# A decode block with cached attention and a gated MLP: x in eight loads, W_o in three, and the gate products on h itself

## The chip, the cores and the metric

The kernel runs on one core of one Trainium2 chip. The core has a matrix engine (PE), three engines for elementwise work (DVE, ACT and POOL), a queue engine (SP) that issues most of the loads, and 16 DMA engines that carry them out. The metric is the device time of one execution in microseconds.

## The reference

Two tokens (B = 2, one position each) of width 512 go through one block. The attention has 32 heads of width 128, each with its own cached keys and values of 8192 positions:

```python
h = x + attention(layernorm(x)) @ wo
#   q = layernorm(x) @ wq;  p = softmax(q k / sqrt(128));  attention = p v
n = layernorm(h)
gate = n @ W_gate;  up = n @ W_up          # 512 -> 1376
out = h + (gate * (gate > 0) * up) @ W_down
```

Everything comes in as bfloat16. Keys and values are 268 MB of the 281 MB that the kernel reads; W_q and W_o are 4.2 MB each, and the three MLP weights 1.4 MB each.

## The kernel before, in words

The order of all instructions on every engine is the order of the program text (a manual schedule). The framework adds the waits. It gives each DMA one of eight completion semaphores, named DMAHW0 to DMAHW7, in turn; a DMA that takes a semaphore again is preceded by a wait for the DMA that had it before.

*Front.* x comes in as five small loads issued by ACT (L190), each a piece of one token's row in one partition. SP issues W_q, the first K tile and the first V tile right behind each other (L193, L165). x is transposed on PE, `ln_cols` (L169) makes its layernorm, and 32 products (L252) make q, which is spread over the partitions as `qrep`. DVE meanwhile reduces the identity matrix into small selection matrices `quot` and `rest` (L243, L244).

*Caches.* Four heads of one token are a step: a K tile and a V tile of 8 MB each, in three rotating buffers of 8 MB. In each step DVE multiplies most of K by q (`products`, L375) and adds up by halves (`scores`, L393 and L395), while PE and ACT do the rest of the rows (`scores_pe`); the exponentials follow, and PE multiplies them by V (`values`, L446). SP issues the next V when the scores have freed K's buffer and the next K but one when `values` has freed V's buffer. The last four heads of the second token are two half steps, p0 and p1, of 4 MB tiles; p1's values are taken with V as the weights (`values_cols`, L469), in two halves.

*W_o.* The attention result of a head is a column `ocol` of 128 values. For a set of n heads, `spread` and `lay_rows` (L492, L496) lay these columns out in `orow` so that W_o can be read with n * 512 values of consecutive rows in each partition, and `attend_set` (L502) multiplies them. Before, the sets are 16, 8, 4 and 2 heads (`SETS`), and the last two heads (HM = 30 and 31), which come last from p1, are loaded one by one and multiplied without the layout, by `attend` (L509). That makes six loads of W_o (L567, L589, L590). The first is issued ahead of p1's V, the others right behind it.

*MLP.* W_gate, W_up and W_down follow in SP's queue (L612, L616, L621), W_down in seven pieces. `hc` (L659) is h in columns, in float32. Its mean is a product with a constant matrix (L661), `hn` is h minus its mean in bfloat16 (L666), and `through` (L686) multiplies 11 chunks of 128 rows of W_gate by `hn`. The variance is applied behind the products. Meanwhile h is split into three bfloat16 parts `hb` (L674 to L677), which PE transposes into `hrow` (L695) for adding h back. Then come W_up's products, `hm` (L727), the products with W_down (`down`, L719), two copies and the store (L736).

Of the kernel before, what the change touches and what calls it, by code (L numbers as in the profile page):

```python
# [8 lines left out]
ALU = mybir.AluOpType  # L9
AXIS = mybir.AxisListType  # L10
# [3 lines left out]
def _free(t, offset, dims):  # L14

    return bass.AP(tensor=t.tensor, offset=t.offset + offset, ap=[t.ap[0]] + [list(d) for d in dims])


def _dram(t, offset, dims):
    return bass.AP(tensor=t.tensor, offset=t.offset + offset, ap=[list(d) for d in dims])  # L20
# [3 lines left out]
def kernel(  # L24
# [13 lines left out]
    nc = tc.nc  # L38
    P = nc.NUM_PARTITIONS
    B, Sq, D = A_x.shape  # L40
    _, Hkv, Sk, Dh = A_k_cache.shape
    Hq = A_wq.shape[1] // Dh
    F = B_W_gate.shape[1]
    KC = D // P
    EPS = 1e-5
    SCALE = float(Dh) ** -0.5
    bf16 = mybir.dt.bfloat16
    f32 = mybir.dt.float32
# [16 lines left out]
    QZ = 32  # L65


    SETS = [(0, 16, 0), (16, 8, 16), (24, 4, 24), (28, 2, 28)]
    HM = 30
    SROWS = [n for _, n, _ in SETS]  # L70


    FSETS = [(0, 5), (5 * P, 3), (8 * P, 1), (9 * P, 1), (F - P, 1)]
    FC = 11
# [7 lines left out]
    consts = ctx.enter_context(tc.tile_pool(name="consts", bufs=1))  # L82
    small = ctx.enter_context(tc.tile_pool(name="small", bufs=1))
    ps = ctx.enter_context(tc.tile_pool(name="ps", bufs=1, space=PSUM))
    ps2 = ctx.enter_context(tc.tile_pool(name="ps2", bufs=2, space=PSUM))

    qTs = front.tile([P, B, Hq], bf16)
    ocol = front.tile([P, Hq, B], bf16)
# [16 lines left out]
    ident = consts.tile([P, P], bf16)  # L105
# [3 lines left out]
    mean_w = consts.tile([P, P], f32)  # L109
    eps_col = consts.tile([P, 1], f32)  # L110
    warm = consts.tile([P, 1], f32)
    hm = consts.tile([P, FC, B], bf16)
    quot = {r: consts.tile([P, Dh // r], bf16, name=f"quot{r}") for r in SROWS}
    rest = {r: consts.tile([P, r], bf16, name=f"rest{r}") for r in SROWS}
    orow = [consts.tile([P, r, B], bf16, name=f"orow{k}") for k, r in enumerate(SROWS)]
    sel = consts.tile([B, B, P // 2], bf16)
    xc = consts.tile([P, B, KC], f32)
# [7 lines left out]
    wo = bufs[0][:, HALF:TILE]  # L125
# [60 lines left out]

    with tc.manual_schedule():

        for b, k, n in ((0, 0, 2), (0, 2, 2), (1, 0, 2), (1, 2, 1), (1, 3, 1)):
            nc.scalar.dma_start(  # L190
                out=xr[b:b + 1, k * P:(k + n) * P], in_=_dram(A_x, b * D + k * P, [[D, 1], [1, n * P]]),
            )
# [46 lines left out]
        nc.vector.tensor_copy(xc, x_ps.rearrange("p c b -> p b c"))  # L239
        xn = small.tile([P, KC, B], bf16, tag="xn")  # L240
        ln_cols(xc, xn.rearrange("p c b -> p b c"), "l1")
        for r in SROWS:
            nc.vector.tensor_reduce(out=rest[r], in_=_free(ident, 0, [[1, r], [r, P // r]]), axis=AXIS.X, op=ALU.max)  # L243
            nc.vector.tensor_reduce(out=quot[r], in_=_free(ident, 0, [[r, P // r], [1, r]]), axis=AXIS.X, op=ALU.max)  # L244
        nc.scalar.activation(out=warm, in_=eps_col, func=ACT.Exp)
# [230 lines left out]
        def spread(k, b):  # L476

            h0, n, _ = SETS[k]
            nq = Dh // n
            sp = qrep[:, B * k + b, :]  # L480
            nc.vector.tensor_tensor(
                out=_free(sp, 0, [[nq, n], [1, nq]]), in0=_free(ocol, h0 * B + b, [[B, n], [0, nq]]),
                in1=_free(quot[n], 0, [[0, n], [1, nq]]), op=ALU.mult,
            )
            return sp

        def lay_rows(k, sps, scalar=False):

            r = SROWS[k]
            or_ps = ps.tile([P, B, r], f32, tag="mx")  # L490
            for b in range(B):
                nc.tensor.matmul(out=or_ps[:, b, :], lhsT=sps[b], rhs=rest[r], start=True, stop=True)  # L492
            if scalar:
                nc.scalar.activation(out=orow[k], in_=or_ps.rearrange("p b c -> p c b"), func=ACT.Copy)
            else:
                nc.vector.tensor_copy(orow[k], or_ps.rearrange("p b c -> p c b"))  # L496

        def attend_set(k, r0=0, r1=None):
            for c0 in range(r0, SROWS[k] if r1 is None else r1):
                for c in range(KC):  # L500
                    at = (SETS[k][2] + c0) * D + c
                    nc.tensor.matmul(  # L502
                        out=att_ps[:, c, :], lhsT=_free(wo, at, [[KC, P]]), rhs=orow[k][:, c0, :],
                        start=(k == 0 and c0 == 0 and c == 0), stop=False, skip_group_check=True,
                    )

        def attend(h):
            for c in range(KC):
                nc.tensor.matmul(  # L509
                    out=att_ps[:, c, :], lhsT=_free(wo, h * D + c, [[KC, P]]), rhs=ocol[:, h, :],  # L510
                    start=False, stop=(h == Hq - 1), skip_group_check=True,
                )

        place_q(steps[0])
        for i in range(Q):
# [70 lines left out]
        load_tile(A_v_cache, p1, p1.vt)  # L586
        for k in range(1, len(SETS)):
            load_set(k)
        nc.sync.dma_start(out=wo[:, HM * D:(HM + 1) * D], in_=_dram(A_wo, HM * Dh * D, [[D, P], [1, D]]))  # L589
        nc.sync.dma_start(  # L590
            out=wo[:, (HM + 1) * D:Hq * D], in_=_dram(A_wo, (HM + 1) * Dh * D, [[P // 4 * D, 4], [D, P // 4], [1, D]]),
        )
        scores(p0)

        def first():
# [24 lines left out]
            fc = f0 // P  # L620
            nc.sync.dma_start(out=wd_sb[:, fc:fc + n, :], in_=_dram(B_W_down, f0 * D, [[n * D, P], [1, n * D]]))  # L621
        late = bufs[1][:, HALF + D:HALF + D + P + D]
        hrow, parts3 = late[0:3 * B, 0:D], late[0:3 * B, D:D + B]
        hb = late[:, D + 32:D + 32 + 3 * B * KC].rearrange("p (c k b) -> p c k b", c=KC, k=3)
        hlow = late[:, D + 64:D + 64 + 2 * B * KC].bitcast(f32).rearrange("p (c b) -> p c b", c=KC)
        nb = heads(Q)[2]
        rzs[Q] = small.tile([P, nb], f32, tag="both", name="both")
# [9 lines left out]
        diagonals(Q)  # L637
        exponentials(p1)
        normalise(Q)
        sps = [[spread(k, b) for b in range(B)] for k in range(1, len(SETS))]  # L640
        nc.gpsimd.tensor_tensor(out=parts3, in0=ident[0:3 * B, 0:B], in1=ident[0:3 * B, B:2 * B], op=ALU.add)  # L641
        nc.gpsimd.tensor_tensor(out=parts3, in0=parts3, in1=ident[0:3 * B, 2 * B:3 * B], op=ALU.add)
        half = p1.nt // 2
        values_cols(p1, 0, half)
        for k in range(1, len(SETS)):
            lay_rows(k, sps[k - 1])
        nc.vector.memset(wd_sb[0:AGAIN, FC - 1, :], 0.0)
        sums(Q + 2)
        shares(Q + 2)
        values_cols(p1, half, p1.nt)  # L650
        normalise(Q + 2)
        for k in range(1, len(SETS)):
            attend_set(k)
        for h in range(HM, Hq):
            attend(h)

        nc.vector.tensor_tensor(out=hc, in0=att_ps.rearrange("p c b -> p b c"), in1=xc, op=ALU.add)  # L659
        m_ps = ps.tile([P, B, KC], f32, tag="mx")  # L660
        nc.tensor.matmul(out=m_ps, lhsT=mean_w, rhs=hc, start=True, stop=True)  # L661
        mean = small.tile([P, B], f32, tag="l1mean")
        nc.vector.tensor_reduce(out=mean, in_=m_ps, axis=AXIS.X, op=ALU.add)
        hn = small.tile([P, KC, B], bf16, tag="hn")
        mean_b = _free(mean, 0, [[1, B], [0, KC]])
        nc.vector.tensor_tensor(out=hn.rearrange("p c b -> p b c"), in0=hc, in1=mean_b, op=ALU.subtract)  # L666
        dev = small.tile([P, B, KC], f32, tag="l1dev")
        nc.vector.tensor_tensor(out=dev, in0=hc, in1=mean_b, op=ALU.subtract)
        sq = small.tile([P, B, KC], f32, tag="l1sq")
        nc.vector.tensor_tensor(out=sq, in0=dev, in1=dev, op=ALU.mult)  # L670


        hcc = hc.rearrange("p b c -> p c b")
        nc.vector.tensor_copy(hb[:, :, 0, :], hcc)  # L674
        nc.vector.tensor_tensor(out=hlow, in0=hcc, in1=hb[:, :, 0, :], op=ALU.subtract)
        nc.vector.tensor_copy(hb[:, :, 1, :], hlow)
        nc.vector.tensor_tensor(out=hb[:, :, 2, :], in0=hlow, in1=hb[:, :, 1, :], op=ALU.subtract)  # L677

        chunks = [(f0 + c, n) for f0, n in FSETS for c in range(n)]
        UP = 5  # L680

        def through(w_ps, k, part, cs=range(KC)):
            for fc in part:
                f0, n = chunks[fc]
                for c in cs:
                    nc.tensor.matmul(  # L686
                        out=w_ps[:, fc - part[0], :], lhsT=_free(wgu[:, k, c, :], f0, [[n, P]]), rhs=hn[:, c, :],
                        start=(fc == part[0] and c == 0), stop=(c == KC - 1), skip_group_check=True,
                    )

        g_ps = ps.tile([P, FC, B], f32, tag="row")
        through(g_ps, 0, range(FC))
        hT_ps = ps2.tile([3 * B, KC, P], bf16, tag="o")
        for c in range(KC):
            nc.tensor.transpose(hT_ps[:, c, :], hb[:, c].rearrange("p k b -> p (k b)"), ident)  # L695
        nc.scalar.activation(
            out=hrow.rearrange("q (p c) -> q p c", c=KC), in_=hT_ps.rearrange("q c p -> q p c"), func=ACT.Copy,
        )
        v_ps = ps.tile([P, B, KC], f32, tag="mx")
        nc.tensor.matmul(out=v_ps, lhsT=mean_w, rhs=sq, start=True, stop=True)  # L700
        rvar = small.tile([P, B], f32, tag="l2rvar")
        nc.vector.tensor_reduce(out=rvar, in_=v_ps, axis=AXIS.X, op=ALU.add)
        nc.vector.tensor_scalar_add(rvar, rvar, EPS)
        nc.vector.reciprocal(out=rvar, in_=rvar)
        gate = small.tile([P, FC, B], f32, tag="gate")
        nc.vector.scalar_tensor_tensor(
            out=gate, in0=g_ps, scalar=0.0, in1=_free(rvar, 0, [[0, FC], [1, B]]), op0=ALU.max, op1=ALU.mult,
        )
        parts = [(range(0, UP), "of", ps), (range(UP, FC), "tp", ps2)]
        u_ps = [pool.tile([P, len(part), B], f32, tag=tag, name="u_ps") for part, tag, pool in parts]  # L710
# [11 lines left out]
                )  # L722

        for t, (part, _, _) in zip(u_ps, parts):
            through(t, 1, part)
            f = slice(part[0], part[-1] + 1)
            nc.vector.tensor_tensor(out=hm[:, f, :], in0=gate[:, f, :], in1=t, op=ALU.mult)  # L727
        down(parts3, hrow, start=True)
# [38 lines left out]
```

## Time and profile before

| | |
|---|---|
| runs | 659.56, 658.91, 659.28 us; median 659.28 |
| span of the profiled execution | 657.5 us, 1.8 us less than the median of the runs |
| busy: DVE, PE, PE weight loads, ACT, POOL | 558.1, 352.1, 158.9, 123.6, 24.1 us |
| read from HBM | 281.05 MB, 427 GB/s over the span |
| share of the loads' queue in the time of 16 DMA engines | 99.1% |

The span begins with the first recorded instruction and ends with the last. "SPq" and "ACTq" are DMA issues by SP and ACT. A line `start length engine line op out<-in xcount [idle before <-releaser]` is one group of instructions in order of time. The chain that ended last is followed back from the end, from each step to what released it; a piece `DMA tile<-in_...` in it lasts from the load's issue to its landing, including the time in which it stood behind other loads.

### The profile page before, as it was taken

To read this page: it belongs to the slowest core of one execution; us is meant where nothing else is said; L and a number is where in the kernel's file an instruction comes from. 1 tells how busy PE (TensorE), PEld (TensorE's weight loads), DVE (VectorE), ACT (ScalarE), POOL (GpSimd) and SP (SyncE) were. 2 spreads that over 40 slices of the span, in tenths; PEclk is the share of its full clock that TensorE was granted. 3 is DMA by queue.
4 is the path that set the end of the run, shared out by engine and by line. 5 is a ranking of instruction groups with operands and counts; after the bars stand their busy time and mean duration, and the time that the engine had idled before them with its cause. 6 is when DMAs were issued, how large, how long until landed. Compare 5 with 4: busy or idle time off the path is not lost.

```text
span 657.5 us, 5117 instructions
## 1 busy us (share of the span) xinstructions
PE 352.1 (54%) x2118; PEld 158.9 (24%) x2118; DVE 558.1 (85%) x252; ACT 123.6 (19%) x337; POOL 24.1 (4%) x36
## 2 busy tenths in 40 slices
PE   0730934809175380926539092552918458291997
PEld 0310311304022130312204031220403224030456
DVE  0599697988979799897979989796997969999982
ACT  0230030200203020030301103030210304201870
POOL 3080000000000000000000000000000000000020
PEclk9975775958778596877959687695968869686895
DMA  9999999999999999999999999999999999999997
GB/s 383 447 444 447 387 440 443 447 399 444 439 443 436 419 436 435 439 439 436 423 443 424 439 440 427 447 416 443 439 423 440 423 443 436 423 444 413 425 425 291
DMA packets 6948, 281.37 MB, mean 428 GB/s; under 512 B 809, under 2 KB 1422, under 8 KB 1934
## 3 DMA queue, kind: packets, MB, share of 16 engines
q1 hardware_dynamic: 6916, 281.06, 99.1%
q8 instruction: 16, 0.26, 0.1%
q14 instruction: 6, 0.05, 0.0%
q10 hardware_dynamic: 10, 0.00, 0.0%
HBM read 281.05 MB, written 0.00 MB: 427 GB/s over the span
## 4 chain that ended last, share of the span: by engine, by line
DVE 42%; DMA 37%; PE 18%; ACT 1%; issue 1%; ACTq 0%; SPq 0%; DVEq 0%
DMA tile<-in_A_k_cache_dram 30%; DVE tile L375 19%; DVE tile L393 18%; PE pv_ps L446 16%; DMA tile<-in_A_wo_dram 4%; DVE scol L395 2%; DMA tile<-in_A_x_dram 2%; DMA tile<-in_B_W_down_dram 1%; PE q_ps L252 1%; DVE pgq L420 1%; ACT ecol L415 1%; DVE pm L399 1%; DVE qrep L395 0%; DVE pm L410 0%; DVE hmax L412 0%
## 5 line engine op out<-in xcount | busy, mean ns | idle before, releaser
L446 PE MATMUL pv_ps<-tile,pgq 128*16 128x512 bf16 x960 | 244.3, 421 | 235.8 <-DVE pgq L420 223.2
L375 DVE TENSOR_TENSOR tile<-tile,qrep 128x29696 bf16<-128x29696 bf16 (+3 forms) x16 | 232.4, 14524 | 44.9 <-DMA tile<-in_A_k_cache_dram 44.9
L393 DVE TENSOR_TENSOR tile<-tile 128x14848 bf16<-128x14848 bf16 (+7 forms) x68 | 236.4, 3477 | 2.2
L446 PEld LDWEIGHTS <-pgq 128*16 128x16 bf16 x960 | 91.6, 97 | 378.1 <-DVE pgq L420 234.5
L451 ACT ACTIVATE pv<-pv_ps 16x512 f32<-16x512 f32 (+1 forms) x16 | 9.4, 589 | 243.7 <-PE pv_ps L446 243.6
L350 ACT ACTIVATE tile<-t_ps 128x1024 bf16<-128x1024 bf16 x53 | 52.6, 1022 | 12.6 <-PE t_ps L349 12.1
L415 ACT ACTIVATE ecol<-scol,nmax 128x256 bf16<-128x256 f32 x14 | 7.1, 508 | 196.1 <-DVE nmax L414 196.1
L340 PE MATMUL row_ps<-tile,qz 128*24 128x512 bf16 (+1 forms) x98 | 30.1, 389 | 18.0 <-ACT tile L350 17.9
L349 PE MATMUL t_ps<-ident,tile 128*128 128x128 bf16 x424 | 32.3, 229 | 13.0 <-DMA tile<-in_A_k_cache_dram 13.0
L349 PEld LDWEIGHTS <-tile 128*128 128x128 bf16 x424 | 25.8, 103 | 28.1 <-issue 14.2
L395 DVE TENSOR_REDUCE scol<-tile 128x232 f32<-128x1856 bf16 (+1 forms) x14 | 28.9, 2067 | 0.5
L641 POOL TENSOR_TENSOR tile<-ident 6x2 bf16<-6x2 bf16 x1 | 2.1, 2147 | 583.5 <-ACT tile L381 583.5
L420 DVE TENSOR_TENSOR pgq<-ecol,ownb 128x1024 bf16<-128x1024 bf16 x15 | 10.4, 692 | 10.3 <-ACT ecol L415 10.3
L381 ACT ACTIVATE tile<-tile 128x128 bf16<-128x128 bf16 x60 | 17.6, 293 | 1.9 <-DVE tile L375 1.9
L281 POOL COPY qzp<-qTs 128x4 bf16<-128x4 bf16 x1 | 15.0, 14982 | 26.1 <-DVE qTs L276 26.1
L375 DVE TENSOR_TENSOR tile<-tile,qpair 128x4096 bf16<-128x4096 bf16 (+3 forms) x4 | 15.5, 3883 | 0.0
L340 PEld LDWEIGHTS <-qz 128*24 128x24 bf16 (+1 forms) x98 | 7.9, 92 | 27.6 <-issue 22.7
L239 DVE CAST xc<-x_ps 128x8 f32<-128x8 bf16 x1 | 0.2, 167 | 15.5 <-PE x_ps L238 15.5
L367 ACT ACTIVATE scol<-sc_ps 32x24 f32<-32x24 f32 (+1 forms) x56 | 11.7, 209 | 7.7 <-PE sc_ps L362 7.2
L362 PE MATMUL sc_ps<-ident_f,tile 24*128 24x24 f32 (+2 forms) x68 | 7.2, 220 | 11.1 <-ACT tile L358 11.1
L358 ACT ACTIVATE tile<-row_ps 24x512 f32<-24x512 f32 (+2 forms) x17 | 10.0, 586 | 13.5 <-PE row_ps L340 13.5
L381 ACT ACTIVATION_READ_ACCUMULATOR tile<-tile 128x1 f32 x60 | 11.2, 186 | 0.0
(133 smaller groups left out, 143.8 us busy)
## 6 DMA issues: line engine op xcount, KB each, us to landing
tile<-in_A_k_cache_dram SPq DMA_DIRECT2D x2, 4096.0 KB
tile<-in_A_v_cache_dram SPq DMA_DIRECT2D x2, 4096.0 KB, 19.6
tile<-in_A_wq_dram SPq DMA_DIRECT2D x1, 4096.0 KB, 12.2
tile<-in_A_wo_dram SPq DMA_DIRECT2D x1, 2048.0 KB
tile<-in_B_W_gate_dram SPq DMA_DIRECT2D x1, 1376.0 KB, 22.8
tile<-in_B_W_up_dram SPq DMA_DIRECT2D x1, 1376.0 KB
tile<-in_A_wo_dram SPq DMA_DIRECT2D x1, 1024.0 KB, 23.8
tile<-in_B_W_down_dram SPq DMA_DIRECT2D x1, 640.0 KB
```

The source lines that it names most:

```text
L281: nc.gpsimd.tensor_copy(qzp[:, :, 6:8], qTs[:, B - 1, Hq - NH:Hq].rearrange("p (k j) -> p k j", j=2),)
L340: nc.tensor.matmul(out=row_ps, lhsT=z, rhs=s.kt[:, (nv + c0 + k) * Dh:(nv + c0 + k + 4) * Dh], start=(u == 0), stop=(u == U - 1),)
L349: nc.tensor.transpose(t_ps[:, k, :], s.kt[:, t * Dh:(t + 1) * Dh], ident)
L350: nc.scalar.activation(out=s.kt[:, (nv + c0) * Dh:(nv + c0 + TPC) * Dh], in_=t_ps.rearrange("p t s -> p (t s)"), func=ACT.Copy,)
L367: nc.scalar.activation(out=scols[s.i][r, nv:s.nt].rearrange("p (u t) -> p t u", t=4), in_=sc_ps[r, :, :, j], func=ACT.Copy,)
L375: nc.vector.tensor_tensor(out=kv, in0=kv, in1=_free(s.qr, 0, [[0, n], [1, Dh]]), op=ALU.mult)
L381: nc.scalar.activation(out=kv, in_=kv, func=ACT.Copy, accum_out=scols[s.i][:, t:t + 1])
L393: nc.vector.tensor_tensor(out=lo, in0=lo, in1=hi, op=ALU.add)
L395: nc.vector.tensor_reduce(out=scol[:, s.na:s.nv], in_=_free(s.kt, s.na * Dh, [[Dh, s.nv - s.na], [1, 8]]), axis=AXIS.X, op=ALU.add,)
L415: nc.scalar.activation(out=ecol, in_=scols[s.i], func=ACT.Exp, scale=SCALE, bias=nmax, accum_out=zs[:, s.b, s.g:s.g + 1],)
L420: nc.vector.tensor_tensor(out=s.pg, in0=_free(ecol, 0, [[VG, s.nt // VG], [0, NH], [1, VG]]), in1=_free(ownb, 0, [[0, s.nt // VG], [VG, NH ...
L446: nc.tensor.matmul(out=pv_ps[s.i][r, :], lhsT=s.pg[:, u].rearrange("p j t -> p (j t)"), rhs=s.vt[:, u * VG * Dh:(u + 1) * VG * Dh], start= ...
```

## The change

Four things change.

- x is loaded by eight loads of 128 values, not five of 128 or 256.
- W_o's sets are 16, 8 and 8 heads: three loads in place of six. The last two heads go through the layout like the others, so `attend` and its eight products are gone; the last set's rows for the second token are spread after p1's values, and its `lay_rows` stands between products of the set before. `quot` and `rest` are made for two sizes, not four.
- The gate products take h in two bfloat16 parts (the high part and what it leaves) beside a column of ones: five columns in place of two. The mean times the column of ones' result, which is the sum of each row of W_gate, is subtracted behind the products, in float32. The up products take `hn` as before.
- The order on DVE and PE behind h follows from this: the two parts first, then the mean, `dev`, `sq`, the third part, `hn`; on PE the variance's product ahead of the transposes.

```diff
-    SETS = [(0, 16, 0), (16, 8, 16), (24, 4, 24), (28, 2, 28)]
-    HM = 30
+    SETS = [(0, 16, 0), (16, 8, 16), (24, 8, 24)]
     SROWS = [n for _, n, _ in SETS]
+    LATE = len(SETS) - 1
+    HI, LOW, ONE, LEAST, PARTS = 0, B, 2 * B, 2 * B + 1, 3 * B + 1
...
-        for b, k, n in ((0, 0, 2), (0, 2, 2), (1, 0, 2), (1, 2, 1), (1, 3, 1)):
+        for b, k, n in [(b, k, 1) for b in range(B) for k in range(KC)]:
             nc.scalar.dma_start(
...
-        for r in SROWS:
+        for r in sorted(set(SROWS)):
...
-        nc.sync.dma_start(out=wo[:, HM * D:(HM + 1) * D], in_=_dram(A_wo, HM * Dh * D, [[D, P], [1, D]]))
-        nc.sync.dma_start(
-            out=wo[:, (HM + 1) * D:Hq * D], in_=_dram(A_wo, (HM + 1) * Dh * D, [[P // 4 * D, 4], [D, P // 4], [1, D]]),
-        )
...
-        hrow, parts3 = late[0:3 * B, 0:D], late[0:3 * B, D:D + B]
-        hb = late[:, D + 32:D + 32 + 3 * B * KC].rearrange("p (c k b) -> p c k b", c=KC, k=3)
+        hrow, parts3 = late[0:PARTS, 0:D], late[0:PARTS, D:D + B]
+        hb = late[:, D + 32:D + 32 + PARTS * KC].rearrange("p (c q) -> p c q", c=KC)
...
-        sps = [[spread(k, b) for b in range(B)] for k in range(1, len(SETS))]
+        sps = [[spread(k, b) for b in range(B if k < LATE else B - 1)] for k in range(1, len(SETS))]
...
+        nc.gpsimd.memset(hb, 1.0)
         half = p1.nt // 2
         values_cols(p1, 0, half)
-        for k in range(1, len(SETS)):
+        for k in range(1, LATE):
             lay_rows(k, sps[k - 1])
...
         normalise(Q + 2)
-        for k in range(1, len(SETS)):
+        sps[LATE - 1].append(spread(LATE, B - 1))
+        for k in range(1, LATE - 1):
             attend_set(k)
-        for h in range(HM, Hq):
-            attend(h)
+        attend_set(LATE - 1, 0, SROWS[LATE - 1] - 2)
+        lay_rows(LATE, sps[LATE - 1])
+        attend_set(LATE - 1, SROWS[LATE - 1] - 2)
+        attend_set(LATE)
...
+        nc.vector.tensor_copy(hi, hcc)
+        nc.vector.tensor_tensor(out=hlow, in0=hcc, in1=hi, op=ALU.subtract)
+        nc.vector.tensor_copy(low, hlow)
...
-        g_ps = ps.tile([P, FC, B], f32, tag="row")
-        through(g_ps, 0, range(FC))
+        g_ps = ps.tile([P, FC, ONE + 1], f32, tag="row")
+        through(g_ps, 0, range(FC), hb[:, :, 0:ONE + 1])
+        v_ps = ps.tile([P, B, KC], f32, tag="mx")
+        nc.tensor.matmul(out=v_ps, lhsT=mean_w, rhs=sq, start=True, stop=True)
...
+        nc.vector.tensor_tensor(
+            out=shift, in0=_free(g_ps, ONE, [[ONE + 1, FC], [0, B]]), in1=_free(mean, 0, [[0, FC], [1, B]]), op=ALU.mult,
+        )
+        gate = small.tile([P, FC, B], f32, tag="gate")
+        nc.vector.tensor_reduce(
+            out=gate, in_=_free(g_ps, 0, [[ONE + 1, FC], [1, B], [B, 2]]), axis=AXIS.X, op=ALU.add,
+        )
+        nc.vector.tensor_tensor(out=gate, in0=gate, in1=shift, op=ALU.subtract)
```

## The prediction

> **What bounds the kernel now.** I read the page's slices first, then the busy time by stage, then the chain that ended last, then the tail in order of time. By stage (columns: window, its length, busy time and count of PE, PEld, DVE, ACT, POOL, the granted TensorE clock, the share of the 16 DMA engines, GB/s):
>
> ```profile
> 0.00:4.00 4.00, 0.00 (x0) 0.00 (x0) 0.00 (x0) 1.28 (x1) 3.19 (x18) 1.00 0.69 230
> 32.00:600.00 568.00, 294.64 (x1482) 125.89 (x1479) 507.86 (x171) 89.55 (x182) 14.98 (x1) 0.75 1.00 432
> 640.00:650.00 10.00, 8.45 (x233) 8.09 (x231) 2.64 (x17) 0.00 (x0) 0.00 (x0) 0.50 1.03 416
> 650.00:654.00 4.00, 3.61 (x82) 2.97 (x83) 1.02 (x6) 0.59 (x1) 0.00 (x0) 0.50 0.70 267
> ```
>
> The DMA engines are full from about 2 us, where the first packets start, until 650; in the 568 us of the caches they are 100% busy at 432 GB/s, while DVE has 508 us of work in them. So the transfers are the bound, and a hole in their stream anywhere before 650 us has nothing later that could fill it.
>
> The chain of waits (start, us, what) seems to tell of other things:
>
> ```profile
> 2.11 12.96 DMA tile<-in_A_x_dram
> ...
> 30.96 41.50 DMA tile<-in_A_k_cache_dram
> 72.46 0.02 issue
> 72.48 15.64 DVE tile L375
> ```
>
> It goes through x, the layernorm, q and the issue of the second K tile at 30.96. But 41.5 us is twice what 8 MB takes at 432 GB/s (19.4 us): that load stood behind the first K and V tiles, which SP had issued at once:
>
> ```profile
> 0.74 0.39 SPq L193 DMA_DIRECT2D tile<-in_A_wq_dram  x1
> 1.19 0.41 SPq L165 DMA_DIRECT2D tile<-in_A_k_cache_dram  x1
> 1.66 0.42 SPq L165 DMA_DIRECT2D tile<-in_A_v_cache_dram  x1
> 30.96 0.33 SPq L165 DMA_DIRECT2D tile<-in_A_k_cache_dram  x1
> ```
>
> W_q takes 12.2 us from issue to landing (the page's sixth part), so it lands at 12.96; the packet records show its last packets ending at 12.0 to 12.6 and K's first ones starting at 12.0, with no gap. The first K tile lands 31.1 us after its issue, at 32.3. The tail, last, PE's order of time and the end of the chain of waits:
>
> ```profile
> 651.33 1.58 PE L686 MATMUL u_ps<-hn,tile 128*128 128x2 bf16 x44 [0.30 <-DMA tile<-in_B_W_up_dram]
> ```
>
> ```profile
> 644.18 9.77 DMA tile<-in_B_W_down_dram
> 653.94 0.04 issue
> 653.99 0.60 PE d_ps L719 x15
> 654.61 0.33 PE d_ps L719 x4
> ```
>
> The up products wait for W_up, landed at 651.29; the down products wait for pieces of W_down, the last of which lands at 654.57 by the trace's landings. From there to the end of the span it is 2.97 us. So both ends of the kernel, too, are set by transfers.
>
> **The change, part by part.**
>
> *x by eight loads.* Its cost isn't at x. The built program gives each DMA the next of eight semaphores in turn, and an instruction that takes a semaphore again waits for the landing of the DMA that had it before. Before, five x loads, W_q, K and V used exactly the eight, and the first K and V waited for nothing. With eight x loads the turn is: x, W_q, six x (all eight used), and then the eighth x load waits for the first, K for W_q, V for the second x load. SP's built order of the changed kernel:
>
> ```
> 1 L196 DMACopy tile_79<-in_A_wq_dram 128x16384
> 2 L168 DMACopy tile_77<-in_A_k_cache_dram 128x32768 [waits DMAHW1_49]
> 3 L168 DMACopy tile_78<-in_A_v_cache_dram 128x32768 [waits DMAHW2_49]
> ```
>
> DMAHW1 is W_q's. K, which was queued at 1.19, is now issued when W_q has landed, at 12.96, some 0.07 us of reaction later (SP's issue at 643.73 follows a landing at 643.66). Queued behind it on SP are V and all later loads; the ring, which had 16 MB waiting, is empty. Price, by the row of W_q itself, a load into an idle ring with packets of the same size: 12.2 us for 4.19 MB, of which the stream needs 9.7 at 432 GB/s, so 2.5 us for starting and landing. K's 8.39 MB then take 2.5 + 19.4 = 21.9 and land at 12.96 + 0.07 + 21.9 = 34.9, not 32.3: **+2.6**. From below, by the nearest smaller rows: the first x load landed 1.22 us after its issue, the output 1.15 us after its own; with 1.15 for 2.5 it is **+1.3**. A gain is excluded, since the same bytes follow a later start. I take **+2.5**, close to W_q's row, which is the same kind of load; a tenth off because the first issue of all took 0.39 us on SP and later ones 0.33.
>
> The Trainium skill (DMA: Bandwidth & Descriptors, "Why a DMA increments its semaphore by 16 and not by 1") asks for one semaphore for each transfer in flight, since two that share one cannot be told apart; this rule speaks against a ninth early load, and the built wait obeys it; no run here shows what sharing one would do. The same page ("Anatomy of one DMA", for the gpsimd path) fits about 2.0 us of fixed cost to a transfer; by it the term would be +2.1 with the reaction, against the 2.5 us of W_q's row.
>
> x itself: the five loads landed at 1.96, 7.74, 10.19, 12.62 and 15.07, 2.45 us apart, which is two 32 KB packets of 1.21 us, one before the data and one before the semaphore. Now only W_q's packets are in the way; the loads left when these end, at 12.6, run free, so I expect x at about 13, 2 us earlier. If K's packets got between them, the last would land at 12.62 + 4 x 2.45 = 22.4, and DVE would start its first products at 39.8. Either is worth nothing: the second K tile only has to be issued before V's packets end, at 50.7 + 2.5, and the second V (64.5 now, 7.4 later at the worst) before that K's end, at 72.5 + 2.5.
>
> *Fewer reduces for quot and rest.* Four of 0.27 to 0.38 us leave DVE at 18 to 20 us, where it then waits for q anyway: 0.
>
> *W_o in three loads.* Three issues of 0.42 us leave SP at 618.5 to 620.4, where the ring holds 10 us of work: 0. In the ring, per engine: the last 2 MB were 8 packets of 0.309 us, 8 of 0.159, 8 of 0.084 and 16 of 0.046, together 5.15; now 16 of 0.309, 4.94. But packets overlap a little: by landings, the last 2 MB took 5.04 on the slowest engine, and 1 MB in large packets 2.54, so two such 5.08. Between -0.2 and 0: I take **-0.1**. All that follows in the ring (gate, up, down) moves with it.
>
> *The last heads by rows.* Out of PE's stretch between the halves of values_cols go two of three lay_rows (each about 0.45 us, with its copy on DVE), so the second half starts some 0.9 us earlier. Behind it come a spread on DVE (0.2), a lay_rows (0.4) and its copy, covered by 32 of the same 64 products. The sum h, at 646.98 now, comes about 0.5 earlier against the stream.
>
> *Gate from h itself.* Its 44 products wait for three DVE operations of 0.17 to 0.2 us behind h (0.65) instead of the mean and its subtraction (1.1), then for W_gate, landed at 647.6. Five columns instead of two cost nothing that the rows show (products of 2 and 8 columns both run 0.1 or less apiece). Behind them DVE has three more operations of about 0.2 on 128x22 to 128x44, PE the same v_ps and transposes. PE would be free for W_up's products at about 650.6 in the old timing, DVE have the gate at 650.9; W_up lands at 651.2. All of this is covered, with some 0.6 us to spare, and buys nothing: next late is W_up, then W_down's last piece. Without that cover, each 0.1 us there would count in full. The POOL memset and the 7-row parts run beside DVE's adds at 631 to 635: 0. The later loads' semaphores turn out harmless: W_up no longer waits for W_o, and W_down's pieces stand behind W_up in the ring as before.
>
> Sum on the profiled execution: 657.5 + 2.5 - 0.1 = 659.9 of span. The median of the runs is 1.8 above that span, which I add unchanged: 659.28 + 2.4 = **661.7**.
>
> **The rivals.**
>
> *Cheap restart.* The ring starts again in the 1.15 us of the small rows: 659.28 + 1.3 - 0.2 = 660.4, within 0.2% (which is 1.3 us, about what a measurement of this kernel can tell from no change). For it: W_q's first packets may be slow only because nothing had run. Against: 16 engines with 32 KB packets are not a 2 KB store. 0.08.
>
> *Faster through x.* If the front is what the chain says, x two us earlier moves q, the second K's issue and everything behind it: 659.28 - 2.0 - 0.1 = 657.2. Against it: the second K tile's issue finds 20 us of V still to come. It would decide only if that issue came after V's end at 50.7, and it comes at 31. 0.03.
>
> *Faster through fewer loads.* The Trainium skill (the same page, "Rules for kernel authors") advises few large transfers, the fixed cost being paid by each; the trace bears this out little, as the landings below tell. As a mechanism here: each of the three W_o loads removed gives back a fixed time in the ring. At 1.15 us each it is 3.4, more than K's wait: 659.28 + 2.5 - 3.4 = 658.4. It decides from 0.83 us a load. Against: the landings of the W_o loads on one engine follow each other by 1.24, 0.63, 0.34 and 0.37 us, in proportion to their bytes. 0.02.
>
> *Slower still.* The tail's cover fails (the longer DVE sequence, or the last rows waiting for W_o) by up to 0.7 us: 662.4. It counts within the forecast's range.
>
> **How the numbers follow.** Slower by 2.2 to 2.8 us is 0.87 with its neighbours above; the cheap restart 0.08; the two faster cases 0.05. The range takes in the cheap restart's price at its low end (660.4) and the failing cover at its high end (662.4); the two faster cases stay out. So faster 0.05, same 0.08, slower 0.87.
>
> **What would show it.** SP's issue of the first K tile at about 13 us and DVE's first products at 34.5 to 35, not 32.4; the DMA share of 13 to 15 us well under 1, and 1.00 after it; x's transposes at 13, not 15.2; W_up's products still waiting for their load, near 653.7, with PE idle about 1 us before them, and the last W_down piece at 657. Wrong, if the first products start before 34, if the stream shows a new hole elsewhere, or if PE reaches W_up's products after the load has landed.

## The result, and the profile after

| kernel | median us | runs | ratio to the kernel before (95% interval) |
|---|---|---|---|
| before | 659.28 (658.91 to 659.79) | 5 | 1 |
| changed | 661.93 (661.49 to 662.31) | 5 | 1.0038 (1.0026 to 1.0050) |

The changed kernel is slower by 2.65 us; 661.7 was forecast. The span of its profiled execution is 660.0 us, 2.5 more than before.

By stage (columns as in the prediction's first fence), the changed kernel:

```profile
0.00:4.00 4.00, 0.00 (x0) 0.00 (x0) 0.00 (x0) 0.66 (x1) 3.19 (x18) 1.00 0.71 229
...
12.00:14.00 2.00, 0.29 (x4) 0.21 (x4) 0.12 (x1) 0.00 (x0) 0.00 (x0) 1.00 0.39 132
...
32.00:600.00 568.00, 293.07 (x1478) 125.44 (x1478) 505.82 (x169) 89.36 (x181) 0.00 (x0) 0.75 1.00 433
```

The DMA engines are as full as before from 32 to 600 us, at 433 GB/s against 432. The new thing is the stretch from 12 to 14 us, with a share of 0.39. SP's order of time in the changed kernel says why:

```profile
0.73 0.38 SPq L196 DMA_DIRECT2D tile<-in_A_wq_dram  x1
13.02 0.33 SPq L168 DMA_DIRECT2D tile<-in_A_k_cache_dram  x1
13.40 0.42 SPq L168 DMA_DIRECT2D tile<-in_A_v_cache_dram  x1
30.06 0.33 SPq L168 DMA_DIRECT2D tile<-in_A_k_cache_dram  x1
```

K is issued at 13.02, not 1.19: W_q's last engine landed at 13.00. In the packet records the engines end W_q between 12.1 and 12.7, nearly as before, but K's first packets start at 14.0 to 14.9, and 15 of the 16 take 2.8 to 3.3 us where later ones of that size take 2.42 in the median. On average an engine is idle for 1.8 us and then 0.6 us slower. K lands at 34.62, 2.36 later than before, and DVE's first products start 2.31 later:

```profile
34.72 15.09 DVE L378 TENSOR_TENSOR tile<-tile,qrep 128x28672 bf16<-128x28672 bf16 x1 [3.21 <-DMA tile<-in_A_k_cache_dram]
```

x itself comes earlier, and the second K tile is issued earlier (30.06, not 30.96), yet it lands later, as the chain of the changed kernel shows (start, us, what):

```profile
3.06 10.45 DMA tile<-in_A_x_dram
...
30.06 44.59 DMA tile<-in_A_k_cache_dram
...
74.82 15.64 DVE tile L378
```

The chain still runs through x, landed at 13.50 and not 15.07. Of the 1.6 us gained there, 0.9 are left when the second K tile is issued, and they are lost in the next DMA piece, which grew from 41.50 to 44.59 us: the load stands behind a K and a V that started later. At the end of the kernel, PE's order of time:

```profile
649.99 1.58 PE L684 MATMUL g_ps<-tile,tile 128*128 128x5 bf16 x44 [0.56 <-DMA tile<-in_B_W_gate_dram]
653.77 1.58 PE L684 MATMUL u_ps<-hn,tile 128*128 128x2 bf16 x44 [1.24 <-DMA tile<-in_B_W_up_dram]
```

and the end of the chain:

```profile
649.96 7.07 DMA tile<-in_B_W_down_dram
657.03 0.04 issue
657.07 0.33 PE d_ps L725 x4
```

PE now waits 1.24 us for W_up, not 0.30: the tail's computation did become shorter against the stream. The last piece of W_down lands at 657.03, 2.46 after the 654.57 of before, and from there to the end it is 2.98 us, as before (2.97). Of these 2.46 us, 2.36 stand between W_q and K already.

### The profile page after: what moved, and what is told of

It reads as the page before. It is cut to its first block, busy times and chain, and to the rows that moved or that the text cites. A ratio compares the mean times of both kernels' runs of the same rounds, so it can differ in the third digit from the quotient of the medians.

```text
span 660.0 us, 5112 instructions
## 1 busy us (share of the span) xinstructions
PE 352.6 (53%) x2116; PEld 159.5 (24%) x2116; DVE 557.4 (84%) x248; ACT 123.6 (19%) x337; POOL 8.7 (1%) x37
## 4 chain that ended last, share of the span: by engine, by line
DVE 42%; DMA 37%; PE 19%; ACT 1%; issue 1%; ACTq 0%; DVEq 0%
DMA tile<-in_A_k_cache_dram 30%; DVE tile L378 19%; DVE tile L396 18%; PE pv_ps L449 17%; DMA tile<-in_B_W_gate_dram 4%; DVE scol L398 2%; DMA tile<-in_A_x_dram 2%; PE q_ps L255 1%; DMA tile<-in_B_W_down_dram 1%; DVE pgq L423 1%; ACT ecol L418 1%; DVE pm L402 1%; ACTq L193 0%; DVE qrep L398 0%; DVE pm L413 0%
## 5 line engine op out<-in xcount | busy, mean ns | idle before, releaser
L255 PE MATMUL q_ps<-tile,xn 128*2 128x512 bf16 x32 | 9.6, 465 | 1.0 <-DVE xn L188 1.0
L365 PEld LDWEIGHTS sc_ps<-ident_f,tile 24*128 24x128 f32 (+2 forms) x68 | 5.5, 136 | 19.4 <-ACT tile L361 19.4
## 6 DMA issues: line engine op xcount, KB each, us to landing
tile<-in_A_wq_dram SPq DMA_DIRECT2D x1, 4096.0 KB, 12.3
```

The costliest lines, as they stand in the source:

```text
L255: nc.tensor.matmul(out=q_ps, lhsT=xn[:, c, :], rhs=wq_sb[:, c, n0:n0 + 4 * Dh], start=(c == 0), stop=(c == KC - 1),)
L365: nc.tensor.transpose(sc_ps[:, t].rearrange("p u j -> p (u j)"), rows[:, t * P:(t + 1) * P], ident_f[0:nh * U, 0:nh * U],)
```

## The experiments

The theory: the eight x loads use up the eight semaphores, so that K waits for W_q, and this hole passes through to the end undiminished. Rival 1: the cost sits in the tail. Rival 2: each x load costs something by itself.

**x back in five loads, and x in eight alone**

```diff
-        for b, k, n in [(b, k, 1) for b in range(B) for k in range(KC)]:
+        for b, k, n in ((0, 0, 2), (0, 2, 2), (1, 0, 2), (1, 2, 1), (1, 3, 1)):
```

> The changed kernel with x in the old five loads; all else as changed. Theory (the first K load waits for W_q's landing and leaves a hole in the stream): K is issued at 1.2 us again, first products at 32.4, last W_down piece near 654.5, time 2.4 to 2.6 us below the changed kernel, 659.2 to 659.5. Rival 1 (the cost sits in the tail: the longer gate sequence, the last heads by rows, W_o's loads): no gain, 661.9. Rival 2 (each x load costs by itself, through the one DMA engine that carries it): also about 659.3, so this run tells theory and rival 2 from rival 1 only.

Measured: 659.57 us, 1.0004 of before (0.9995 to 1.0013). From 12 to 14 us its stream has no hole:

```profile
12.00:14.00 2.00, 0.00 (x0) 0.00 (x0) 0.00 (x0) 0.00 (x0) 0.00 (x0) 1.00 1.21 524
```

(A packet is counted where it starts, hence a share over 1.) The other way round, the kernel before with eight x loads:

> The kernel before with x in eight loads and nothing else. Theory: K issued at 13.0 us, first products at 34.7, time 2.3 to 2.7 us above before, 661.6 to 662.0. Rival 1 (tail): 659.3. Rival 2 (each load costs): 661.6 to 662.0 as well.

Measured: 662.26 us, 1.0047 (1.0034 to 1.0059), 0.3 us above the expectation; K is issued at 12.98. The x loads alone make the whole loss, within the intervals. All the rest of the change together is worth +0.04% by the first run (-0.05 to 0.13), and by the second, set against the whole change (1.0038), about -0.1%: nothing that these runs tell from zero. Rival 1 falls.

**Seven and nine loads**

```diff
-        for b, k, n in [(b, k, 1) for b in range(B) for k in range(KC)]:
+        for b, k, n in ((0, 0, 2), (0, 2, 1), (0, 3, 1), (1, 0, 1), (1, 1, 1), (1, 2, 1), (1, 3, 1)):
```

> The changed kernel with x in seven loads (the first of 256 values, six of 128). By the turn of the eight semaphores K then waits for the first x load, landed at 1.9 us, and V for W_q, while K's packets still fill the ring. Theory: no hole behind W_q, K issued at about 2.1; x lands later, at 12.6 + 3 x 2.45 = 20, so the second V is issued at 69.4 with first packets at 70.4, when the first engines run dry at 70.2: 0 to 0.3 us above five loads, 659.2 to 659.7. Rival 2 (each load costs a third of 2.5 us): 660.9 to 661.1. Rival 1: 661.9.

Measured: 665.51 us, 1.0093 (1.0079 to 1.0107), far from what any of the three expected. Nine loads, the first piece of x cut in two:

> The changed kernel with x in nine loads (two of 64 values, seven of 128). K then waits for the second x load, at about 7.7 us, while W_q still fills the ring; the ninth x load waits for W_q. Theory: no hole behind W_q, but x lands last of all, at 12.6 + 5 x 2.45 = 24.9, the first products start at 41 to 42, the second V is issued at about 74, after the ring ran dry at 70.2 to 72: a new hole of 3 to 5 us there, in all 3 to 4 us above five loads, 662.3 to 663.3. Had the ring's slack no end, it would be 659.3. Rival 2 (each load costs): 662.7. Rival 1: 661.9. The trace tells them apart by where the DMA share falls below 1: at 70 to 75 us by the theory.

Measured: 673.33 us, 1.0218 (1.0204 to 1.0232), ten us over the expectation, though the hole is where it was expected. SP's order of time has K and the second V:

```profile
7.83 0.33 SPq L168 DMA_DIRECT2D tile<-in_A_k_cache_dram  x1
...
81.63 0.33 SPq L168 DMA_DIRECT2D tile<-in_A_v_cache_dram  x1
```

So K's issue moves with the number of x loads as the turn of the semaphores has it: at 1.17 us with five, 1.97 behind the landing of the first x load with seven, 13.02 behind W_q's with eight, 7.83 behind the second x load's with nine. With seven loads K's early issue was foreseen, and there is no hole at 12 us. The hole is at 70 us; by stage, and SP's next V:

```profile
70.00:72.00 2.00, 0.00 (x0) 0.00 (x0) 1.95 (x2) 0.00 (x0) 0.00 (x0) 0.50 0.00 0
```

```profile
40.77 0.33 SPq L168 DMA_DIRECT2D tile<-in_A_k_cache_dram  x1
74.19 0.33 SPq L168 DMA_DIRECT2D tile<-in_A_v_cache_dram  x1
```

x landed at 24.8, not at 20, so q, the first products (42.1) and the scores that free K's buffer came late, and the ring, the line of packets waiting for the DMA engines, ran dry from about 70.2 until V's packets started at 75. An engine was idle for 4.9 us on average, and the time is 5.9 above five loads. The size I had wrong is that of K's packets. Up to 12.3 us x's packets and their semaphore writes follow each other by 1.22 us, one 32 KB packet of W_q; behind that by 2.42 us, one 64 KB packet of K, so a load costs 4.85 us and not 2.45. With nine loads this goes on until x lands at about 32, V is issued at 81.6, and the engines are idle for some 12 us, on average from 70.8 to 82.8.

The row was there to be read in the kernel before: its last x load's data came right behind the semaphore of the one ahead (12.30 after 12.29), and its own semaphore not 1.2 but 2.43 us later, at 14.73, as long as one packet of K takes. The prediction took that load's 2.45 us for two packets of 32 KB like the others.

**K and V in rows of 32 KB** tests that reading: seven x loads, and the first K and V in two loads each, with packets of 32 KB.

```diff
-        load_tile(A_k_cache, steps[0], steps[0].kt)
-        load_tile(A_v_cache, steps[0], steps[0].vt)
+        load_tile(A_k_cache, steps[0], steps[0].kt, 2)
+        load_tile(A_v_cache, steps[0], steps[0].vt, 2)
```

> The changed kernel with x in seven loads, and the first K and V tiles each in two loads, so that a partition's row in one load is 32 KB as in W_q and not 64 KB. With seven loads, x's packets behind W_q were 2.43 us apart and x landed at 24.8. Theory (an x packet waits for one row of the bulk load on its DMA engine: two 32 KB packets for K's rows, one for W_q's): with 32 KB rows the packets stay 1.21 us apart to the end, x lands at about 20, the second V is issued at 69.3, just as the ring runs dry: 659.5 to 660.1. Rival (behind W_q it is two packets for another reason, such as the number of loads queued): x at 24.8 and 665.5 as with seven loads and whole tiles.

Measured: x's packets stay 1.22 us apart to the last (17.05, 18.27), x lands at 18.6, and V is issued early again:

```profile
68.88 0.33 SPq L168 DMA_DIRECT2D tile<-in_A_v_cache_dram  x1
```

That shows the packets' size as the cause of the spacing. The time is 661.87 us, 1.0032 (1.0017 to 1.0047), between the two expectations and within neither, and its runs lie from 659.35 to 664.57, wider than those of any other kernel here. V's issue falls within 2 us of the ring's end, so small differences decide how large the hole is; in the profiled run of 662.71 us about a fifth of the engines' time is idle from 70 to 72 us. By the packet records the idle time around 70 us (0.5 us in the mean of the engines) and the slow packets behind it (0.9) are 1.4 of the 2.7 us by which this run's span is above that with five loads. Another 1.0 are slow packets at 144 to 154 and 222 to 232 us, behind V tiles issued at 147.00 and 224.45, as if the ring had all but run dry there again. That this is all of the spread between the runs was not shown.

**x in two loads**

```diff
-        for b, k, n in [(b, k, 1) for b in range(B) for k in range(KC)]:
+        for b, k, n in [(b, 0, KC) for b in range(B)]:
```

> The changed kernel with x in two loads, one for each token. No semaphore comes round before the first K and V are issued; x lands at 7.7 us, 7.3 earlier than in the kernel before, so that q waits only for W_q at 13. Theory (the stream is the bound; what counts is that it has no hole): the same as five loads, 659.3 to 659.7, with the second K tile issued 5 us earlier and landing no earlier than 72. Rival (the chain of waits is right that x sets the front): 5 to 7 us below five loads, 652 to 655.

Measured: 659.59 us, 1.0003 (0.9994 to 1.0011), the same as five loads. The chain of this kernel:

```profile
25.70 46.90 DMA tile<-in_A_k_cache_dram
...
72.72 15.64 DVE tile L378
```

The second K tile is issued 5.3 us earlier than in the kernel before, and its load "lasts" 5.4 us longer. Behind a full ring the earlier issue bought nothing here, and the chain's path through x is no cause. Rival 2 falls too: two loads are no faster than five, and seven are 3.6 us slower than eight. What a load costs depends on what waits for it.

**More work ahead of the up products.** The variance's product is repeated, with the same operands and result.

```diff
-        nc.tensor.matmul(out=v_ps, lhsT=mean_w, rhs=sq, start=True, stop=True)
+        for _ in range(3):
+            nc.tensor.matmul(out=v_ps, lhsT=mean_w, rhs=sq, start=True, stop=True)
```

> The changed kernel with the variance's product behind the gate products made three times instead of once (the result is the same; 1.0 to 1.2 us more on PE ahead of the up products). Theory: PE waits 1.24 us for W_up there, so this is covered: 0 to 0.2 us above the changed kernel, 661.9 to 662.1. Rival B (PE's chain sets the end): plus 1.2, 663.1.

Measured: 661.80 us, 1.0037 (1.0024 to 1.0049): covered. With five products:

> The same with five such products instead of one: 2.0 to 2.4 us more on PE. Theory: the cover of 1.24 us is used up and the rest counts in full: plus 0.8 to 1.2 us, 662.7 to 663.1. Rival B: plus 2.4, 664.3. Rival C (everything here lies under the stream, whose last piece sets the end): 661.9.

Measured: 661.72 us, 1.0036 (1.0023 to 1.0048): covered too, against my theory and with rival C. (The addition was smaller than expected, 1.71 us and not 2.0 to 2.4; the theory would still have had 0.5 us more.) PE's order of time in that kernel:

```profile
651.46 2.28 PE L693 MATMUL v_ps<-sq,mean_w 128*128 128x8 f32 x10
653.67 0.59 PE L696 MATMUL hT_ps<-ident,tile 128*7 128x128 bf16 x4
654.19 1.58 PE L684 MATMUL u_ps<-hn,tile 128*128 128x2 bf16 x44
655.70 0.27 PE L726 MATMUL d_ps<-tile 7*2 7x128 bf16 x4
655.90 1.38 PE L726 MATMUL d_ps<-tile,hm 128*2 128x128 bf16 x44
```

The products grew from 0.57 to 2.28 us and took up the wait for W_up. The up products start 0.4 us later than in the changed kernel, and the down products win that back: they run through in 1.38 us, where in the changed kernel they took 1.88 with waits for pieces of W_down between. They end at 657.28, level with the last landing (656.95) plus four products. So the cover was the wait for W_up and about 0.5 us of waits for W_down, 1.7 in all, and it is just used up. The kernel before with three products:

> The kernel before with the variance's product made three times instead of once: 1.0 to 1.2 us more on PE, where PE waits 0.30 us for W_up. Theory: plus 0.7 to 0.9 us, 660.1 to 660.3; with the run of the changed kernel with the same addition this shows the cover that the change gains in the tail. Rival B: plus 1.2, 660.6. Rival C: 659.4.

Measured: 659.26 us, 0.9999 (0.9990 to 1.0008), again as rival C had it and not the theory: 0.9 us more work lies under the stream there as well. The change's shorter tail therefore adds cover where there was some already.

No version beat both kernels: with two or five x loads the change stands level with the kernel before, and no run points to one that would be clear of it.

## Why the prediction was right

- *K waits for W_q.* Foreseen at 13.03 us, seen at 13.02. By the row of W_q, K was to land at 34.9; it landed at 34.62, so the term was 2.36 and not 2.5 or 2.6. From issue to first packet it was 0.95 us and the first packets took some 0.6 us longer, much as at W_q's own start (1.0 and 0.7). The lower bound from small loads (1.3) was the wrong row to go by. The 2.0 us of fixed cost that the Trainium skill (DMA: Bandwidth & Descriptors, "Anatomy of one DMA") has for the gpsimd path, with the reaction an estimate of 2.1, comes nearly as near from the other side.
- *Nothing fills the hole.* The stream ran at 433 GB/s behind it, and its last landing moved by 2.46. The removal of the x loads alone brought the time back to 1.0004 of before.
- *x earlier, and worth nothing.* At 13.50 for about 13; shown outright by two loads, with q 5 us earlier and the time unchanged. The side remark was wrong: had K's packets come between, x would not have been at 22.4 but later, since K's packets are of 64 KB. I had taken W_q's packet for all packets. Nor would a late x have been worth nothing: with seven loads x at 24.8 cost 5.9 us, since the engines run dry from about 70.2 and the prediction had gone by the landing of the last one, 72.5. It changed nothing here only because eight loads hold K back until x has passed.
- *W_o in three loads.* I took -0.1. By landings, the last 2 MB of W_o took 5.17 us on the last engine (5.04 before) and 4.87 on the first (5.07 before); with x in five loads the last engine took 4.86. The profiles do not tell this from nothing, and neither do the times. That the sum came within 0.2 us is in part luck: the wait was taken 0.1 too large, and the gain of 0.1 taken here did not show.
- *The tail covered.* Right in its sign and in what is late next: W_up, then W_down's last piece, 2.98 us before the end. The size was off on the safe side. I gave 0.6 us of spare time and let everything beyond count in full; 1.7 us more on PE cost nothing. The step that was missing: the down products, too, stop for their loads, and run faster when they start later.
- *h earlier against the stream.* Foreseen 0.5, measured 0.8 (648.62 is 1.64 behind the 646.98 of before, in a stream that is 2.4 late).
- The rivals: the cheap restart is out, both faster cases are refuted by the two-load run and by the even balance of the rest of the change.

## What to carry to other kernels

When every engine's loads take their completion semaphores in turn from a small set, count the loads issued before the first wait: a load more on a side queue can make the main stream's next load wait for the one before it, and in a kernel bound by its stream such a hole is paid in full however far it is from the end (here 2.36 us behind W_q and 2.46 at the last landing, 620 us later). Read the chain of waits beside the DMA share: a piece that lasts twice as long as its bytes need was standing in a queue, and here what came before it on the chain was not a cause. Small loads beside a bulk stream are priced in the bulk's packets, so merge them; two loads had x in place before it was needed.

## What the runs showed of the hardware that I had not expected

A small load from ACT's queue (in the packet records one packet of data and one write of 4 bytes) waits for one bulk packet before its data and for another before its semaphore: 1.22 us each behind packets of 32 KB, 2.42 behind 64 KB. The Trainium skill (DMA: Bandwidth & Descriptors, "Queues, rings and completion order") has the engines take turns between queue rows by whole packets, and these spacings agree.

The 16 engines do not end together: the last piece of W_down lands from 653.43 to 657.03 in the changed kernel, 3.6 us apart, and the kernel's end hangs on the last of them. What makes some engines late was not tried.
